# Linear attention and token/channel mixer on one core: two groups of input loads moved behind the transposing transfers of u in the SyncE queue

## The chip, the cores and the metric

One Trainium2 chip, one of its cores. The time is that of one execution on the device, in microseconds, and the kernel's time is the median of several executions. A profile of one execution gives what each engine did and when.

## What is computed

Eight batches, each of eight heads, 576 rows and head width 64. Linear attention with the feature map elu+1, then a mixer over rows and one over channels. Cut to what matters:

```python
phi = lambda x: np.where(x > 0, x, np.exp(x) - 1.0) + 1.0
kv  = einsum('bhsd,bhse->bhde', phi(k), v);  z = phi(k).sum(axis=2)
x   = einsum('bhsd,bhde->bhse', phi(q), kv) / (einsum('bhsd,bhd->bhs', phi(q), z) + 1e-6)
x   = x.transpose(0, 2, 1, 3).reshape(8, 576, 512)
h   = maximum(x.transpose(0, 2, 1) @ w_tok1, 0) @ w_tok2     # 576 -> 256 -> 576
u   = x + h.transpose(0, 2, 1)
out = u + maximum(u @ w_ch1, 0) @ w_ch2                      # 512 -> 1536 -> 512
```

## The kernel before, in words

A batch n passes through these steps, named as in the code. `load` (line 132) brings q, k and v of one batch from memory, each in two transfers of 576 KB, all issued by SyncE (SP). There are two sets of buffers for raw inputs, but the second is given over to sums of weights early on, so that from batch 2 on every batch uses the same three buffers (`rb`). `phi_exp` (L151, ScalarE), `phi_add` (L157, VectorE) and `phi_end` (L165, VectorE) make phi(q) and phi(k). `vcast` (L176) makes v bf16. `qtr_dma` (L221) is a transfer that transposes phi(q) into `qT`, in two halves. `kv` (L191 on TensorE) makes the small matrices. `nd_all` (L261 on TensorE, L270 to L290 on VectorE) makes x. `mm1` (L312) and `mm2` (L325) are the row mixer, and L337 on VectorE adds x to give u, two row groups at a time. `utr_dma` (L521) transposes u into `uT` by transfer, in two halves: `uta` after the first L337 of a batch, `utb` after the second. The 64 rows of each batch that fill no tile are kept for a pair of batches: `mm2_tails` (L346, with L350 on VectorE) makes `ut`, and `utr_tail_dma` (L526, step `utt`) transposes it into `uTt`.

The channel mixer of batch n is the large work of TensorE: `mm3` (L543), parts of it as `mix_one` (L723), the tail's part as `mm3_tail` (L557), then `pair_product` (L823) for the second matrix, by a scheme with seven block products instead of eight, whose sums are made on VectorE (`row_sums`, L666; `u_sums`, L700). `mm4` of the tail is L583. ACT takes the relu out of the accumulators (L550), and `pair_end` and `pair_put` add u and store.

The order of the work is written by hand. The outer loop goes over n, the batch whose channel mixer runs. `big` lists the pieces of that mixer, and `put(s, fn, ...)` hangs a step of another batch behind piece s: the row mixer of batch n+1, the feature maps of batch n+2, the loads of batch n+3. The list of steps is sorted by s and is stable, so steps of one s keep the order in which they were put. Every engine, and SP too, carries out its own instructions in this written order; an instruction that waits holds everything behind it on its queue. SP issues nearly all loads and all transposing transfers, on one DMA queue (q1 in the profile); POOL issues the stores of results (q0) in the middle of the run.

Two places matter here. The block for n=1 is written out before the loop; the one for n=2 is the first pass of the loop, with `b0 = 12`:

```python
put(16, load_all, 4, "q")          # n=1: ahead of todo["uta"], put at 19, and todo["utb"], at 24
put(25, load_all, 4, "kv")
...
put(b0 + 7, load_all, n + 3, "qv") # n=2: slot 19
at(b0 + 9, "mm2t")                 # slot 21: ut is made
at(b0 + 9, "utt")                  # slot 21: uTt is transposed
```

Of the kernel before, what the change touches and what calls it, by code (L numbers as in the profile page):

```python
# [19 lines left out]
def kernel(  # L20
# [844 lines left out]
    def m4s(n):  # L865
        return [lambda i=i, j=j: pair_product(n, i, j) for i in ORDER for j in range(2)]
# [133 lines left out]
    def steps(n):  # L1000

        out_ = [("kv", lambda: kv(n, range(2)))] if n < 2 else []
        if n == 1:
            puts = [nc.scalar.copy, nc.vector.tensor_copy if n == 1 else nc.scalar.copy]
            out_ += [(f"qt{c}", lambda c=c: qtr(n, c, puts[c])) for c in range(2)]
        for i, rs in enumerate(([0, 1], [2, 3], [4])) if n < 2 else ():
            for g in range(2):
                out_.append((f"nd{i}{g}", lambda g=g, rs=rs: nd(n, g, rs)))
        if n > 1:
            out_.append(("nd", lambda: nd_all(n)))  # L1010
        out_.append(("mm1", lambda: mm1(n)))
        if n > 1:
            out_ += [("mm2a", lambda: mm2(n, [0, 1])), ("mm2b", lambda: mm2(n, [2, 3]))]
            if n % 2:
                out_.append(("mm2t", lambda: mm2_tails(n // 2)))
            out_ += [("uta", lambda: utr_dma(n, [0, 1])), ("utb", lambda: utr_dma(n, [2, 3]))]
            if n % 2:
                out_.append(("utt", lambda: utr_tail_dma(n // 2)))
        return out_

    def run(bigs, fill):
        for i, big in enumerate(bigs):
            big()
            for s, fn in fill:
                if s == i:
                    fn()
        for s, fn in fill:
            assert s < len(bigs)
# [57 lines left out]
    put = lambda s, fn, *a: fill.append((s, lambda: fn(*a)))  # L1086
# [42 lines left out]
    put(24, todo["mm2b"])  # L1129
    put(24, todo["utb"])  # L1130
    put(24, pair_end, 1, "Z", 0, 0, 0)
    put(16, load_all, 4, "q")
    put(25, load_all, 4, "kv")
    put(26, pair_end, 1, "Y", 0, 1, 1)
    put(28, pair_end, 1, "X", 1, 0)
    put(28, pair_put, 1)
# [5 lines left out]
    for n in range(2, B - 1):  # L1142
        p, b = divmod(n, 2)
        tail = int(n == 3)
        mix = n in MIXED
        big = (m3x if mix else m3)(n) + m3t * tail + m4s(n) + m4(p, [8]) * tail
        b0 = 12 + 3 * tail
        todo = dict(steps(n + 1))
        fill = []
        put = lambda s, fn, *a: fill.append((s, lambda: fn(*a)))  # L1150
        at = lambda s, *nms: [put(s, todo.pop(nm)) for nm in nms if nm in todo]

        def phi_at(nm, ex, ad, en):
            for g in range(2):
                if ex is not None:
                    put(ex[g], phi_exp, nm, n + 2, 2 * g, 2)
            for g in range(2):
                put(ad[g], phi_add, nm, n + 2, 2 * g, 2)
                put(en[g], phi_end, nm, n + 2, 2 * g, 2)

        at(1, "nd")
        if n + 2 < B:
            if n > 3:
                phi_at("k", None, (2, 2), (3, 4))
                put(5, load_all, n + 3, "k")
            nm = "k" if n == 3 else "q"
            if mix:
                for which in (3, 4):
                    put(3, u_sums, which, tuc, b)
            if not mix:  # L1170
                phi_at(nm, (7, 7), (8, 9), (9, 10))
            else:
                for g in range(2):
                    put(3, phi_add, nm, n + 2, 2 * g, 2)
                    put(7, phi_exp, nm, n + 2, 2 * g, 2)
            put(10, *((qtr_dma, n + 2) if n != 3 else (load_all, n + 3, "k")))
            if n == 2:
                for g in range(2):
                    put(13, phi_add, "k", n + 2, 2 * g, 2)
        at(7, "mm1")  # L1180
        for s, k0 in ((7 if mix else 11, 0), (11 if mix else 12, 3)):
            for w in (1, 2):
                put(s, row_sums, n, w, k0, 3)
        if mix and n + 2 < B:
            for g in range(2):
                put(7 + 2 * g, phi_end, nm, n + 2, 2 * g, 2)
        if mix:
            for which in (1, 2):
                put(0, u_sums, which, tuc, b)
        if n == 3:  # L1190
            phi_at("q", (12, 13), (13, 13), (14, 14))
            put(15, qtr_dma, n + 2)
        at(13, "mm2a", "uta")
        put(14, row_sums, n, 3, 0, KH)
        put(b0 + 1, pair_copy, 0)
        if n == 2:
            for g in range(2):
                put(b0 + 1, phi_exp, "k", n + 2, 2 * g, 2)
                put(b0 + 2, phi_end, "k", n + 2, 2 * g, 2)
            put(b0 + 4, load_all, n + 3, "k")  # L1200
        at(b0 + 3 - tail, "mm2b", "utb")
        put(b0 + 4 - tail, row_sums, n, 4, 0, KH)
        put(b0 + 4 - tail, pair_end, n, "Z", 0, 0, 0)
        put(b0 + 5, pair_copy, 1)
        if n + 2 < B:
            for g in range(2):
                put(b0 + (5 if n == 2 else 2) + g, vcast, n + 2, g)
        put(b0 + 7, load_all, n + 3, "qv")
        put(b0 + 7, pair_copy, 2)
        if n > 2 and n + 3 < B:  # L1210
            put(b0 + 8, k_exp, n + 3)
        put(b0 + 9, pair_end, n, "X", 1, 1, 2)
        if n == B - 2:
            at(b0 + 6, "mm2t", "utt")
        at(b0 + 9, "mm2t")
        if n + 2 < B:
            put(b0 + 9, kv, n + 2, range(2))
        at(b0 + 9, "utt")
        put(b0 + 11, pair_end, n, "Y", 0, 1, 1)
        if n == B - 2:  # L1220
            for which in (3, 4):
                put(3, u_sums, which, tuc, b)
            put(1, first_sum)
            for which in range(1, 5):
                if which > 1:
                    put((3, 3, b0 + 2)[which - 2], first_sums, which)
                put(b0 + 10, u_sums, which)
        else:
            put(b0 + 13, pair_end, n, "X", 1, 0)
            put(b0 + 13, pair_put, n)  # L1230
        assert not todo, todo
        run(big, sorted(fill, key=lambda e: e[0]))
# [31 lines left out]
```

## Time and profile before

| What | Value |
|---|---|
| median of 8 executions | 250.29 us (249.14 to 251.64) |
| the profiled execution's own time | 250.17 us |
| its span in the profile | 248.4 us |
| TensorE (PE) busy | 237.1 us, 95% |
| VectorE (DVE) busy | 190.8 us, 77% |
| ScalarE (ACT) busy | 139.3 us, 56% |
| GpSimd (POOL) busy | 70.1 us, 28% |
| moved by DMA | 48.39 MB, mean 195 GB/s |
| mean granted TensorE clock | 0.996 |

The span is what the profile covers; 1.8 us of the execution's time lie outside it. A line of the timeline gives start, duration, engine, source line, operation and tiles, and in brackets how long the engine had been idle before it and what ended that. A line of waits gives the sum, the number and the longest. SPq is the issuing of a transfer by SyncE: its duration is not that of the transfer, and a merged line of two issues holds the pause between them. "Landing" is the time from the start of the issue to the last byte's report.

### The profile page before, as it was taken

The page shows a single profiled execution, that of the slowest core. Times are in us where ns is not written, and L with a number is a line of the kernel's source. Part 1 is how long each engine was busy: PE and PEld are TensorE (multiplying, and loading weights), DVE is VectorE, ACT ScalarE, POOL GpSimd, SP SyncE. Part 2 cuts the span into 40 slices and gives each one's busy share as a digit, 9 for nine tenths or more (in the row PEclk, how much of TensorE's full clock was granted, in tenths as well). Part 3 has the DMA queues.
Part 4 walks back from the last instruction along what each step waited for, and adds up shares of the span by engine and source line. Part 5 has one row for each costly group of instructions (what it writes and reads, how often), then busy time and mean ns, then how long its engine had stood idle before and what let it go on. Part 6 is the DMA issues. An engine that isn't in the chain of part 4 may idle for free.

```text
span 248.4 us, 5964 instructions
## 1 busy us (share of the span) xinstructions
PE 237.1 (95%) x2432; PEld 158.1 (64%) x2454; DVE 190.8 (77%) x330; ACT 139.3 (56%) x224; POOL 70.1 (28%) x84
## 2 busy tenths in 40 slices
PE   7699999999999799999899999999999999999993
PEld 3484455554877356875588545765577566888672
DVE  5954778897899698989894398858894879956853
ACT  4764791579765277736797168655952651275100
POOL 9770030496503600070004500051006800430000
PEclk9999999999999999999999999999999999999998
DMA  6999999999528992589949966699052702352036
GB/s 249 261 203 257 352 266 334 330 287 299 232 49 220 246 401 72 120 257 346 311 137 157 404 171 219 121 319 273 22 123 45 164 8 42 63 121 51 4 84 169
DMA packets 49771, 48.39 MB, mean 195 GB/s; under 512 B 30032, under 2 KB 35536, under 8 KB 49744
## 3 DMA queue, kind: packets, MB, share of 16 engines
q1 hardware_dynamic: 41648, 35.00, 48.1%
q0 software_dynamic: 7472, 12.22, 22.4%
q10 hardware_dynamic: 624, 0.79, 1.1%
q8 instruction: 19, 0.31, 0.5%
q14 instruction: 8, 0.07, 0.1%
HBM read 35.85 MB, written 9.44 MB: 182 GB/s over the span
## 4 chain that ended last, share of the span: by engine, by line
PE 59%; DMA 7%; DVE 3%; issue 1%; DVEq 0%
PE ps L823 19%; PE ps L543 15%; DMA uTt<-ut 5%; PE ps L751 4%; PE ps L777 4%; PE ps L312 3%; PE ps L325 3%; PE ps L723 3%; PE ps L570 2%; DMA uT<-u 2%; PE ps L592 2%; PE ps L261 1%; PE ps L191 1%; PE ps L557 1%; PE ps L583 1%
## 5 line engine op out<-in xcount | busy, mean ns | idle before, releaser
L543 PE MATMUL ps<-uT,wc 128*128 128x512 bf16 x284 | 66.5, 379 | 1.6 <-DMA uT<-u 1.3
L550 ACT ACTIVATE cr<-ps 128x512 bf16<-128x512 f32 x67 | 39.1, 600 | 35.6 <-PE ps L543 35.3
L543 PEld LDWEIGHTS <-wc 128*128 128x128 bf16 x288 | 27.3, 98 | 31.2 <-DMA uT<-u 1.8
L834 POOL TENSOR_TENSOR obuf<-obuf,q_raw 128x512 f32<-128x512 f32 x6 | 7.6, 1268 | 93.4 <-DVE obuf L832 60.8
L823 PE MATMUL ps<-k_raw,v_raw 128*128 128x256 bf16 x216 | 24.9, 273 | 0.0
L832 DVE TENSOR_TENSOR obuf<-ps,u 128x512 f32<-128x512 f32 x24 | 16.2, 687 | 10.4 <-PE ps L823 8.9
L823 PEld LDWEIGHTS <-cr 128*128 128x128 bf16 x216 | 21.0, 98 | 4.1
L823 PEld LDWEIGHTS <-v_raw 128*128 128x128 bf16 x216 | 21.0, 98 | 3.9 <-issue 0.4
L151 ACT ACTIVATE e<-q_raw 128x1152 bf16<-128x1152 f32 x16 | 18.3, 1161 | 7.2 <-DMA q_raw<-in_q_dram 7.2
L151 ACT ACTIVATE e<-k_raw 128x1152 bf16<-128x1152 f32 x16 | 18.2, 1165 | 3.5 <-DMA k_raw<-in_k_dram 3.5
L823 PE MATMUL ps<-wc,cr 128*128 128x256 bf16 x144 | 17.7, 273 | 0.0
L666 DVE TENSOR_TENSOR v_raw<-cr 128x768 bf16<-128x768 bf16 (+2 forms) x24 | 14.8, 619 | 3.6 <-ACT cr L729 2.1
L276 DVE TENSOR_TENSOR x<-ps,dens 128x768 bf16<-128x768 f32 x18 | 17.2, 954 | 0.4
L337 DVE TENSOR_TENSOR u<-ps,x 128x1024 bf16<-128x1024 f32 x12 | 14.7, 1222 | 1.9 <-PE ps L325 1.7
L312 PE MATMUL ps<-x,w 128*128 128x512 bf16 x49 | 13.4, 379 | 0.3
L176 ACT CAST vs<-v_raw 128x1152 bf16<-128x1152 f32 x12 | 13.5, 1163 | 0.0
L157 DVE TENSOR_SCALAR y<-k_raw 128x1152 bf16<-128x1152 f32 x16 | 11.7, 762 | 2.1 <-DMA k_raw<-in_k_dram 2.1
L165 DVE TENSOR_TENSOR qp<-e,y 128x1152 bf16<-128x1152 bf16 x16 | 11.9, 755 | 1.0 <-ACT e L151 0.3
L157 DVE TENSOR_SCALAR y<-q_raw 128x1152 bf16<-128x1152 f32 x16 | 12.3, 784 | 0.0
L834 POOL TENSOR_TENSOR obuf<-obuf,part 128x512 f32<-128x512 f32 x6 | 7.6, 1274 | 15.8 <-DVE obuf L832 15.8
L325 PE MATMUL ps<-ar,w2p 128*128 128x512 bf16 x44 | 11.8, 379 | 0.3
L165 DVE TENSOR_TENSOR kp<-e,y 128x1152 bf16<-128x1152 bf16 x16 | 11.7, 751 | 0.5 <-ACT e L151 0.4
(178 smaller groups left out, 428.6 us busy)
## 6 DMA issues: line engine op xcount, KB each, us to landing
k_raw<-in_k_dram SPq DMA_DIRECT2D x16, 576.0 KB, 6.1
q_raw<-in_q_dram SPq DMA_DIRECT2D x16, 576.0 KB, 6.3
v_raw<-in_v_dram SPq DMA_DIRECT2D x14, 576.0 KB, 10.0
out_dram<-obuf POOLq DMA_DIRECT2D x12, 512.0 KB, 6.6
wc<-in_moe_w_ch_dram POOLq DMA_DIRECT2D x8, 384.0 KB, 10.0
out_dram<-obuf POOLq DMA_DIRECT2D x4, 256.0 KB, 5.2
cr<-in_v_dram POOLq DMA_DIRECT2D x2, 288.0 KB, 7.5
out_dram<-obuf POOLq DMA_DIRECT2D x4, 128.0 KB, 7.5
```

Source lines behind the costliest of these rows:

```text
L151: nc.scalar.activation(out=e, in_=f, func=AF.Exp)
L157: nc.vector.tensor_scalar(out=y, in0=f, scalar1=1.0, scalar2=1.0, op0=ALU.add, op1=ALU.max)
L165: live["phi"] = nc.vector.tensor_tensor(out=dst.transpose([0, 2, 1, 3]), in0=e.rearrange("p (i t d) -> p i t d", i=nj, t=T), in1=y.rearran ...
L276: nc.vector.tensor_tensor(out=xv[:, :, rc0:rc0 + 3], in0=v_[m][:, :, k0:k0 + 6, 0:D].rearrange("p i (q a) d -> p i q a d", a=2), in1=den.r ...
L312: nc.tensor.matmul(out=ps[:, mt], lhsT=w1t[:, b, ms] if r == R else w1[:, r, ms], rhs=x[b][:, r, :], start=(r == 0), stop=(r == R))
L325: nc.tensor.matmul(out=ps[:, i], lhsT=w2v(kt, r, b), rhs=ar[b][:, kt, :], start=(kt == 0), stop=(kt == NT - 1 and not add))
L543: nc.tensor.matmul(out=ps, lhsT=wc1[:, kj, 128 * mc:128 * mc + 128], rhs=uTj[b][:, kj] if n < 2 else uT[b][:, :, kj], start=(kj == 0), sto ...
L550: nc.scalar.activation(out=cr[b][:, mc, :], in_=ps, func=AF.Relu)
L666: nc.vector.tensor_tensor(out=s_[which - 1][:, ks], in0=x_, in1=y_, op=op)
L823: nc.tensor.matmul(out=live[tile_][:, j], lhsT=lhs[:, k_], rhs=rhs[:, k_], start=(first and j == 0 and k_ == 0), stop=(k_ == KH - 1), skip ...
L832: nc.vector.tensor_tensor(out=o, in0=live[tile_], in1=u[n % 2][:, d::2, HC[c]], op=ALU.add)
L834: nc.gpsimd.tensor_tensor(out=o, in0=o, in1=part[i], op=ALU.add)
```

## The change

Two groups of loads go further back in SP's queue; no computation changes.

```diff
@@ block n=1
     put(24, todo["mm2b"])
     put(24, todo["utb"])
     put(24, pair_end, 1, "Z", 0, 0, 0)
-    put(16, load_all, 4, "q")
-    put(25, load_all, 4, "kv")
+    put(25, load_all, 4, "qkv")
     put(26, pair_end, 1, "Y", 0, 1, 1)
@@ loop, n from 2
-        put(b0 + 7, load_all, n + 3, "qv")
+        if n != 2:
+            put(b0 + 7, load_all, n + 3, "qv")
         put(b0 + 7, pair_copy, 2)
...
         at(b0 + 9, "utt")
+        if n == 2:
+            put(b0 + 9, load_all, n + 3, "qv")
         put(b0 + 11, pair_end, n, "Y", 0, 1, 1)
```

In the order of SP's instructions this is all that moves: in block n=1 the two loads of q of batch 4 go from ahead of the two transposes of u of batch 2 to behind both; in block n=2 the four loads of q and v of batch 5 go from ahead of the transpose of ut to behind it. PE, DVE, ACT and POOL keep their order.

## The prediction, made before the changed kernel was run

> **What bounds the kernel now.** I read the page first, then the waits of PE, then the timelines of PE and of SP's queue around each wait. PE is busy for 95% of the span at full clock, so only PE's idle time can be won. The waits of PE between 60 and 140 us are:
>
> ```profile
> PE ps L543 <- DMA uT<-u: 1.3, 1, 1.3
> PE ps L557 <- DMA uTt<-ut: 0.6, 1, 0.6
> PE ps L543 <- issue: 0.2, 1, 0.2
> ```
>
> So two transposing transfers hold PE up, once each. The chain of waits names the same two, with larger numbers:
>
> ```profile
> 78.88 5.21 DMA uT<-u
> 111.07 12.16 DMA uTt<-ut
> ```
>
> Those are whole transfers, from issue to landing. The second is almost wholly hidden: PE has other work until the last 0.6 us. What can be won is the idle time in brackets on PE's own timeline:
>
> ```profile
> 80.08 2.76 PE L583 MATMUL ps<-wc,crt 128*128 128x512 bf16 x11
> 84.14 1.90 PE L543 MATMUL ps<-uT,wc 128*128 128x512 bf16 x8 [1.30 <-DMA uT<-u]
> ...
> 122.05 0.60 PE L723 MATMUL ps<-q_raw,wc 128*128 128x256 bf16 x4
> 123.27 1.95 PE L557 MATMUL ps<-uTt,wc 128*128 128x128 bf16 x32 [0.62 <-DMA uTt<-ut]
> ```
>
> SP's timeline shows what stood in front of them:
>
> ```profile
> 75.13 1.13 SPq L132 DMA_DIRECT2D q_raw<-in_q_dram  x2
> 76.35 5.70 SPq L521 DMA_TRANSPOSE uT<-u  x2
> 82.15 1.04 SPq L132 DMA_DIRECT2D k_raw<-in_k_dram  x2
> ...
> 106.35 1.06 SPq L132 DMA_DIRECT2D k_raw<-in_k_dram  x2
> 107.46 2.48 SPq L132 DMA_DIRECT2D q_raw<-in_q_dram  x2
> 110.03 0.93 SPq L132 DMA_DIRECT2D v_raw<-in_v_dram  x2
> 111.07 1.26 SPq L526 DMA_TRANSPOSE uTt<-ut  x1
> ```
>
> By the tile views the two q loads (issued 75.13 and 75.8) took 5.4 and 6.4 us, so they landed at 80.5 and 82.2; the first half of uT, issued 76.35, took 6.9 and landed at 83.25; the second took 5.2 and landed at 84.10. Landings follow the order of issue, and the transposes came in 1 to 2 us after the last q. The DMA view of 76.6 to 80.6 us supports it: 431 of its 512 packets are of load size, though half a transpose had been asked for since 76.35.
>
> ```profile
> DMA packets 512, 1.01 MB, mean 251 GB/s; under 512 B 81, under 2 KB 81, under 8 KB 512
> ```
>
> (the counts by size are sums from below: 81 of the 512 are under 512 B, as a transpose's are). One merged SP line hides more: the second half's issue alone lasted 3.17 us (78.88 to 82.05), where the same issue takes 1.23 to 1.26 us behind an empty queue.
>
> **Part A, block n=1: q of batch 4 behind both halves of uT.** Nothing is added or removed. The two q issues (0.61 and 0.43 us) leave 75.13 and come after the second half.
> Step A1: the first half waits for u, whose first L337 ends at 74.57 + 1.22 = 75.79; it issues at about 75.85. The second waits for L337 ending at 77.64 + 1.22 = 78.86, as before.
> Step A2: with no load in front, its landing is read from the rows of other blocks: 3.1 and 3.1 us (101.69 and 105.0), 3.6 and 3.1 (157.26 and 159.66), 3.0 and 3.0 (182.9 and 185.1); the one at 131.79, close behind two transposes of q, took 5.1. The 159.66 row is nearest: a first half shortly before, q loads issued 1.35 us later. So 78.88 + 3.1 = 82.0, and 84.0 at worst. PE is free at 82.84. The stall of 1.30 us goes, with 0.8 us to spare; by the 5.1 us row only 0.1 of it goes.
> Step A3: what is late next? VectorE's L621 ends at 83.09 + 0.68 = 83.77 and frees a bank that L261 overwrites; L261 comes 1.83 us into PE's new run, at 84.67. The L700 sums (0.42 us each) then run from 83.77 to 84.65, and VectorE is free for L270 when L261 ends at about 85.4. From L270 on VectorE is nearly solid to 109 us, but that run is itself released by PE's L261, so it moves forward whole: PE gains nothing on it. The next half of uT lands at 105.02 + 3.1 = 108.1 against PE's need at 109.48; both move. A gives 1.30.
> Step A4, the price: q is issued at 78.88 + 1.25 = 80.1 and 80.8 instead of 75.13 and 75.8, about 5 us later; k and v behind it keep their place in the data, since all the bytes in front of v are the same. First reader of q:
>
> ```profile
> 91.41 1.42 DVE L157 TENSOR_SCALAR y<-q_raw 128x1152 bf16<-128x1152 f32 x2
> ```
>
> That will be 90.1 after the gain, the second half 90.8. Loads in this stretch took from 5.1 (k, 82.15) to 8.8 us (k's second, 82.75, beside POOL's stores issued from 82.51). So q's second half lands between 87.2 (6.4) and 89.6 us (8.8); I take 87.2, as its data goes ahead of most of the stores. Cost nil, covered by the VectorE work between landing and L157 (nd's L270 to L289 and two L700); if the cover went, each us of lateness first eats 0.88 us of VectorE's idle time (0.42 at 93.25, 0.46 at 98.03) and 1.4 us of uT's margin at 109.48, and then is PE's.
> k and v follow by about 1 us or less: v landed at 94.4 (83.8 + 10.6), read at 103.54; k at 91.5, read at 99.11. The next SP instruction, the transpose of q at 97.64, has an empty queue either way. POOL's queue has nothing moved past it; its stores only share the DMA engines.
>
> The Trainium skill, "DMA: Bandwidth & Descriptors", section "Rules for kernel authors", speaks against A: issue a DMA early and wait on its semaphore late. By that rule taken alone q's 5 us of lead are given away for nothing, and the sum would be 0 at best. The rows say that the lead is not used: q landed at 82.2 and is first read at 91.41, 9 us later, while uT landed 1.30 us too late. The rows decide: 1.30.
>
> **Part B, block n=2: q and v of batch 5 behind uTt.** Four issues of 0.4 to 2.0 us leave the place ahead of the transpose. They now queue behind its wait for ut, whose L350 ends at 106.98 + 1.38 = 108.36.
> Step B1: the transpose issues at 108.4 instead of 111.07, with only k in front, which landed at 107.0 + 5.8 = 112.8. Its own landing: 2.4 us with nothing near it (213.27), 6.7 behind q and v (164.21), so between 112.8 and 115.1. PE needs it at 122.65. The stall of 0.62 us goes with over 7 us to spare, if nothing else stands there: banks and relu of L557 are next. Its second group uses the bank that ACT's L729 empties at 122.74 + 0.59 = 123.33, and PE reaches it at about 123.5. So 0.62, with 0.2 us over.
> Step B2, the price: q issues at about 109.7 (or up to 111.6, if the transpose's issue takes the 3.17 us seen behind loads) instead of 107.46, and v some 2 to 4 us later than 110.03. q landed at 109.5 + 7.4 = 116.9 and would land at 119 to 121; its reader is L157 at 124.43, 122.5 after both gains. v landed at 122.8 and ends at about the same time, as the bytes are the same; its reader is at 128.84. Cost nil; with the cover gone, VectorE's idle times of 0.26 and 0.29 us after L157 are all there is to absorb it.
> k of batch 6 and later transfers keep their order, and wait for work of VectorE at 119.64, not for the queue.
>
> **Sum.** 1.30 + 0.62 = 1.92 us off the span, 248.4 to 246.5; the profiled execution goes from 250.17 to 248.25. The median of the eight was 0.12 above it: 250.29 becomes 248.4.
>
> **The rivals.**
> R1: only one part works. A fails if the transpose meets the 5.1 us row instead of the 3.1 us one: landing at 84.0, PE as late as before. Then only B is left: 250.29 - 0.62 = 249.7. For it: that row also had q loads behind it. Against it: two transposes of q were in front of it, where here the last one lands at 73.7 + 3.6 = 77.3, before the second half is asked for. If instead B's stall passes to the next wait (ACT's bank), A alone gives 249.0.
> R2: nothing. The transposes were slow for a reason other than the loads, or PE's gain is all taken back at the next dependence on VectorE, which is solidly busy from 98.5 to 109. Time 250.3. Against it: VectorE's run starts with PE's L261, and the landings follow the queue's order.
> R3, slower: q of batch 4 comes too late for L157 at 90.1, and VectorE, in order, holds back everything behind it: sums, relus and u. It breaks even where lateness exceeds 0.88 + 1.4 + 1.92 = 4.2 us, that is a landing at 94.3, 13.5 us after issue. The longest q load in the trace took 12.4 us, at the start beside the weights; v in this stretch took 11.5. A landing at 96.5 would give 252.5. It needs stores and loads to halve each other's rate for the whole stretch, and q stands ahead of k and v.
>
> **How the numbers follow.** The change as written, both stalls gone (247.9 to 248.9, with 248.4 likeliest): 0.64. Two small further gains or losses downstream are inside that. R1: A alone 0.07 (half of it over 0.5%), B alone 0.10. R2: 0.07. R3 or another late transfer: 0.12. About 0.5%, 1.25 us, is what a measurement of this kernel can tell from no change. So faster 0.64 + 0.035, about 0.68; same 0.035 + 0.10 + 0.07, about 0.20; slower 0.12. The range runs from 247.7 (below the main case's end, for the spread of 249.1 to 251.6 in single executions) to 250.0, which takes in both forms of R1; R3 and most of R2 lie outside.
>
> **What would show it.** Right: SP issues the second half of uT for about 1.25 us at 78.9; landings of 3.0 to 3.6 us; no DMA wait of PE at L543 or L557; L157's q line with no idle time before it. Wrong in A: a landing over 4 us. Wrong in R3's way: VectorE idle before L157 or ACT before L151 for a load of q. Gone elsewhere: new idle time of PE between 84 and 125 us, released by VectorE or ACT.

## The result, and the profile after

| | before | after |
|---|---|---|
| median | 250.78 us (33 runs, on the chips of this comparison) | 248.40 us (12 runs) |
| ratio of the comparison | | 0.9921, 95% interval 0.9900 to 0.9942 |
| span of the profiled execution | 248.4 us | 246.6 us |

The changed kernel is faster by 0.8%, 2.0 us of 250.78, clear of the 0.5% that can be told from no change. The medians lie 2.4 us apart; the 2.0 follow from the ratio, which leaves out slower executions of the kernel before, such as the four above 253 us.

The waits of PE between 55 and 140 us, where there were two for transfers, are down to one line, in the changed kernel's profile:

```profile
PE ps L543 <- issue: 0.2, 1, 0.2
```

PE's timeline at the two places. The brackets with the waits are gone, and L543 begins before the modelled end of L583 (80.50 + 2.76 = 83.26):

```profile
80.50 2.76 PE L583 MATMUL ps<-wc,crt 128*128 128x512 bf16 x11
83.10 1.89 PE L543 MATMUL ps<-uT,wc 128*128 128x512 bf16 x8
...
120.98 0.60 PE L723 MATMUL ps<-q_raw,wc 128*128 128x256 bf16 x4
121.42 1.95 PE L557 MATMUL ps<-uTt,wc 128*128 128x128 bf16 x32
```

SP's timeline shows the new order, and the loads right behind:

```profile
76.23 4.30 SPq L521 DMA_TRANSPOSE uT<-u  x2
80.62 1.06 SPq L132 DMA_DIRECT2D q_raw<-in_q_dram  x2
81.78 0.93 SPq L132 DMA_DIRECT2D k_raw<-in_k_dram  x2
...
105.29 1.06 SPq L132 DMA_DIRECT2D k_raw<-in_k_dram  x2
107.33 1.51 SPq L526 DMA_TRANSPOSE uTt<-ut  x1
108.89 1.08 SPq L132 DMA_DIRECT2D q_raw<-in_q_dram  x2
110.09 0.92 SPq L132 DMA_DIRECT2D v_raw<-in_v_dram  x2
```

The second half of uT was issued at 79.30 and landed after 3.1 us (5.2 before); uTt landed after 4.7 us (12.2 before). q of batch 4 landed at 84.9 and 86.8, and VectorE reaches it with no bracket, that is, without waiting:

```profile
90.36 1.42 DVE L157 TENSOR_SCALAR y<-q_raw 128x1152 bf16<-128x1152 f32 x2
```

Starts on PE give the account. From L583's start to L543's: 4.06 us before (84.14 - 80.08), 2.60 after (83.10 - 80.50), so 1.46 won. From the last L723 to L557: 1.22 before, 0.44 after, so 0.78 won. That is 2.24; PE reached L583 0.42 us later in this execution, which leaves 1.82 of span. From L557 to the end both profiles are the same to 0.01 us, since PE never waits there.

### The profile page after: what moved, and what is told of

Same layout as the page of the kernel before. It is cut to its first block, busy times and chain, and to the rows that moved or that the text cites. A ratio compares the mean times of both kernels' runs of the same rounds, so it can differ in the third digit from the quotient of the medians.

```text
span 246.6 us, 5963 instructions
## 1 busy us (share of the span) xinstructions
PE 237.7 (96%) x2432; PEld 158.6 (64%) x2454; DVE 190.6 (77%) x330; ACT 139.5 (57%) x224; POOL 70.4 (29%) x84
## 4 chain that ended last, share of the span: by engine, by line
PE 82%; DMA 11%; POOL 3%; issue 1%; DVE 1%; SPq 0%; POOLq 0%
PE ps L823 23%; PE ps L543 21%; DMA wc<-in_moe_w_ch_dram 7%; PE ps L312 6%; PE ps L583 5%; DMA q_raw<-in_q_dram 5%; PE ps L325 4%; PE ps L723 4%; PE ps L751 4%; PE ps L777 4%; PE ps L557 2%; PE ps L570 2%; PE ps L592 2%; PE ps L261 2%; PE ps L191 2%
## 5 line engine op out<-in xcount | busy, mean ns | idle before, releaser
L543 PE MATMUL ps<-uT,wc 128*128 128x512 bf16 x284 | 66.5, 379 | 0.3 <-issue 0.2
L543 PEld LDWEIGHTS <-wc 128*128 128x128 bf16 x288 | 27.4, 98 | 29.7 <-issue 0.9
L823 PE MATMUL ps<-k_raw,v_raw 128*128 128x256 bf16 x216 | 24.9, 273 | 0.0
L823 PEld LDWEIGHTS <-cr 128*128 128x128 bf16 x216 | 21.0, 98 | 4.1
L823 PEld LDWEIGHTS <-v_raw 128*128 128x128 bf16 x216 | 21.1, 98 | 3.9 <-issue 0.4
L823 PE MATMUL ps<-wc,cr 128*128 128x256 bf16 x144 | 17.7, 273 | 0.0
L157 DVE TENSOR_SCALAR y<-k_raw 128x1152 bf16<-128x1152 f32 x16 | 11.7, 763 | 2.3 <-DMA k_raw<-in_k_dram 2.3
L157 DVE TENSOR_SCALAR y<-q_raw 128x1152 bf16<-128x1152 f32 x16 | 12.3, 784 | 0.0
L583 PE MATMUL ps<-wc,cr 128*128 128x512 bf16 x47 | 11.8, 379 | 0.3 <-DMA wc<-in_moe_w_ch_dram 0.3
```

What stands on the lines that cost most here:

```text
L157: nc.vector.tensor_scalar(out=y, in0=f, scalar1=1.0, scalar2=1.0, op0=ALU.add, op1=ALU.max)
L543: nc.tensor.matmul(out=ps, lhsT=wc1[:, kj, 128 * mc:128 * mc + 128], rhs=uTj[b][:, kj] if n < 2 else uT[b][:, :, kj], start=(kj == 0), sto ...
L583: nc.tensor.matmul(out=ps, lhsT=crt[:, kc, :] if t == 8 else cr[b][:, kc, 128 * r:128 * r + 128], rhs=wc2[:, kc, :], start=(kc == 0), stop ...
L823: nc.tensor.matmul(out=live[tile_][:, j], lhsT=lhs[:, k_], rhs=rhs[:, k_], start=(first and j == 0 and k_ == 0), stop=(k_ == KH - 1), skip ...
```

## The experiments

All edits are to the changed kernel unless said otherwise. Each is timed beside the kernel before on the same chip. Starts on PE (L583 to L543, "the gap at L543": 4.06 before, 2.60 without a wait) are compared rather than spans, since the time before 80 us varies by some tenths.

**Each part alone, and both again.** `a_alone` has only the first edit of the diff, `b_alone` only the second.

> Part A only: q of batch 4 behind both halves of uT; q and v of batch 5 stay ahead of uTt. Theory (order in SP's queue, two independent stalls): PE's wait of 1.3 us at L543 is gone, PE's wait of 0.6 us at L557 stays; 1.3 to 1.5 us faster than before, ratio about 0.9945. Rival (the stalls are one delay handed on, so that a start 1.4 us earlier meets uTt that comes no earlier): the wait at L557 grows by up to 1.4 us to about 2.0, and the ratio is about 1.000.

> Part B only: q and v of batch 5 behind uTt; q of batch 4 stays ahead of uT. Theory: PE's wait of 1.3 us at L543 stays, that at L557 goes; 0.6 to 0.8 us faster than before, ratio about 0.997. Rival (the wait at L557 is also one for ACT's bank, which comes no earlier): at most 0.2 us, ratio 0.999 to 1.000.

> Both parts, beside each part alone on the same chip. Theory (independent): the sum of the two, 1.9 to 2.3 us, ratio 0.991 to 0.9925. Rival (they overlap): no better than part A alone, about 0.9945.

Measured on one chip, before at 250.96: part A alone 250.17, ratio 0.9960 (0.9937 to 0.9984); part B alone 250.04, 0.9963 (0.9935 to 0.9991); both 249.06, 0.9940 (0.9918 to 0.9963). The medians give 0.79 + 0.92 = 1.71 us for the parts and 1.90 for both: the parts add up, within the intervals. These are wide: that of both holds the theory's 0.9925 and the rival's 0.9945 alike, and only the first measurement of the change (0.9921) and a third one further down (0.9899) decide for the theory. In the profile of part B alone the wait at L557 is gone and 0.98 us of wait at L543 stays. But two profiles hold something neither theory expected. In that of part A alone, which is that of the slowest of its 22 executions (251.24), PE waits for both:

```profile
83.79 1.90 PE L543 MATMUL ps<-uT,wc 128*128 128x512 bf16 x8 [0.79 <-DMA uT<-u]
124.36 1.95 PE L557 MATMUL ps<-uTt,wc 128*128 128x128 bf16 x32 [2.06 <-DMA uTt<-ut]
```

The wait at L557 grew by 1.44 us, as the rival had it, though uTt did not merely come no earlier: issued at 110.98 it took 13.3 us, and came 1.1 later than in the kernel before. The trace has a fetch of instructions in it (queue q8, one packet of 16 KB), which began at 120.31 and held one of the sixteen DMA engines for 2.66 us. The transpose's last two completions came at 123.38, all others by 122.34, so the fetch accounts for 1.0 of the 1.1. And in the second profile of the changed kernel itself the wait at L543 is back, with no load in front:

```profile
84.06 1.90 PE L543 MATMUL ps<-uT,wc 128*128 128x512 bf16 x8 [0.88 <-DMA uT<-u]
```

The half of uT issued at 79.22 took 4.8 us there. The DMA views from 79.5 to 84 us of the two profiles of this one kernel differ in their counts and in one line, which is in the second only:

```profile
q8 instruction: 1, 0.02, 1.3%
```

A fetch again; it began at 81.98 us and held one DMA engine for 0.94 us, to 82.92. That is where the transpose was being finished: all its other completions came by 81.82, the last two at 82.93, right behind the fetch. Of the sixteen reports that make up the landing fifteen were in by 82.44, the last at 84.01. In the first profile the fetch came at 88.5. The kernel before has no fetch between 73 and 88 us, so its own wait at L543 is not of this kind.

**More and less in front of uT.** `half` leaves one of q's two loads in front, `double` both and k between the halves:

```diff
-    put(25, load_all, 4, "qkv")
+    put(16, load, "q", 4, 0)            # half
+    put(25, load, "q", 4, 1); put(25, load_all, 4, "kv")
+    put(16, load_all, 4, "q")           # double
+    put(23, load_all, 4, "k"); put(25, load_all, 4, "v")
```

> Part B kept; of q of batch 4 one load (half the bytes) ahead of both halves of uT as before, the other behind them. Theory (order in the queue, with a fixed time when PE comes): the one load is done by about 79.5 to 80.5 us, the halves of uT land by 80.5 to 81.5 and 82.0 to 82.6, PE waits 0 to 0.2 us: as fast as both parts within 0.3 us. Rival (delay in proportion to the bytes): half the wait, 0.6 us, stays.

> Part B kept; q of batch 4 ahead of both halves of uT as before, and k of batch 4 between the halves. Theory (order in the queue): the second half lands behind 1.18 MB more, at about 330 GB/s 3.6 us later, at 87 to 88 us; PE waits 4.5 to 5.5 us at L543; 2.5 to 3.5 us slower than before. Rival (sharing of the DMA engines, order without effect): the second half lands less than 2 us later than before, PE waits under 3.3 us, and the time is at most 1.3 us above before.

`half`: ratio 0.9919 (0.9889 to 0.9948), what the changed kernel has. One load in front delays the first half of uT (4.9 us instead of 3.1) and costs nothing that the time shows, because PE comes late enough; but the interval is too wide to exclude the rival's 0.6 us. Its profile has 0.99 us of wait at L543, and a fetch at 82.44. Fifteen of the sixteen reports of the second half were in by 82.94, the last, behind the fetch, at 84.50. PE would have gone on at 80.80 + 2.60 = 83.40: without the fetch there would have been no wait, as the theory has it. `double`: the second half landed 8.6 us after its issue at 79.70, at 88.3, and PE waited as the order of the queue has it:

```profile
88.32 3.59 PE L543 MATMUL ps<-uT,wc 128*128 128x512 bf16 x8 [4.66 <-DMA uT<-u]
```

The time, 255.36 against 251.13 (ratio 1.0169, 1.0108 to 1.0229), is 4.2 us worse, more than the 2.5 to 3.5 expected. The eight matmuls took 3.59 us instead of 1.89. The windows (PEclk is the third number from the end) show why:

```profile
82.00:87.00 5.00, 1.66 (x8) 0.57 (x6) 2.59 (x4) 0.00 (x0) 3.38 (x5) 0.93 1.19 283
87.00:92.00 5.00, 3.68 (x14) 1.19 (x16) 0.85 (x2) 0.65 (x2) 0.00 (x0) 0.50 1.03 384
92.00:94.00 2.00, 2.00 (x45) 1.43 (x42) 1.02 (x3) 0.55 (x1) 0.00 (x0) 0.73 0.89 353
```

After the long idle time PE was granted half its clock, from 86.3 to 93.1 us, which cost another 2.15 us between L543 and the last L723. The Trainium skill, "TensorE: Matmul & The Clock Gate", section "Part 1: The HAM clock gate", has the clock halved after an idle window of about 3.4 us; the rows agree in kind but not in size, as the clock fell 2.6 us after PE's last matmul (83.66). Stalls of up to 2.06 us in the other profiles (`a_alone`, `act_q`) kept the full clock.

**The same bytes on another queue.** `pool_q` has POOL issue q of batch 4, `act_q` ACT; k and v stay behind uT.

```diff
-    put(25, load_all, 4, "qkv")
+    for c in range(2):
+        put(16, load_pool, 4, "q", c)   # nc.gpsimd.dma_start; act_q: slot 24, nc.scalar
+    put(25, load_all, 4, "kv")
```

> Part B kept; the two loads of q of batch 4 issued in their old place (slot 16) but by POOL, so on another DMA queue than the transposes. Theory (the transposes wait for the bytes ahead of them in their own queue): the two queues take turns, the halves of uT land at about 80.5 and 82 to 82.9 us, PE waits 0 to 0.4 us, time within 0.4 us of both parts. Rival (any load in flight takes the DMA engines from the transposes): they land at 83.3 and 84.1 as before, PE waits 1.3 us, time that of part B alone (ratio 0.997).

> Part B; the two loads of q of batch 4 issued by ACT at about 77.4 us, so on another queue than the transposes and in flight beside both halves of uT. Theory (what delays a transpose is mainly the bytes ahead in its own queue): the second half lands 3.1 to 4.2 us after its issue (82 to 83.1), PE waits 0 to 0.3 us without a fetch. Rival (any load in flight delays it, by about its own bytes): it lands at 84 or later, PE waits 1.2 us or more as in the kernel before.

`pool_q`: no wait at L543, gap 2.60, ratio 0.9937 (0.9910 to 0.9965). But it does not tell what it was made for: POOL had nothing else to do and issued at 70.2, so q had landed by 76.6, before the halves of uT were in flight (both took 3.1 to 3.2 us). What those loads did hold up is the transpose of q in front: its issue at 73.80 lasted 2.90 us, until q was in, against 1.31 in the kernel before. `act_q` does tell: q was issued at 76.48 and 77.02, the halves of uT at 77.55 and 80.6.

```profile
86.64 1.90 PE L543 MATMUL ps<-uT,wc 128*128 128x512 bf16 x8 [2.06 <-DMA uT<-u]
```

The first half took 6.7 us, as behind q on SP's own queue (6.9), and landed 1.1 us after q's last byte. The second took 6.0, with a fetch at 84.5 in it; fifteen of its sixteen reports were in after 4.5 us, at 85.09, and PE could have gone on at 84.42, so 0.7 us of the wait is left without the fetch. This execution, 251.91, is the slowest of the run. Time 250.04, ratio 0.9973 (0.9950 to 0.9995), that of part B alone. The rival is right here, if smaller than it said: what delays a transpose is load data in flight, on whichever queue. The change works because q is asked for late enough, not because SP's queue is special.

**How late may q be?** `kqv` and `kvq` only change the order of the loads behind uT.

```diff
-    put(25, load_all, 4, "qkv")
+    put(25, load_all, 4, "kqv")         # or "kvq"
```

> Both parts, but batch 4 is loaded in the order k, q, v. Theory: q lands at 89 to 91 us, L157 at about 90.4 waits 0 to 0.7 us for it, absorbed by VectorE's idle time: the time is that of both parts within 0.3 us. Rival (VectorE has no slack there): what L157 waits shows in the time one for one.

> Both parts, but batch 4 is loaded in the order k, v, q, so that q comes last. Theory (the price of a late q as reckoned before the run: 0.88 us of VectorE's idle time and 1.4 us of uT's margin absorb the first 2.3 us): q lands at about 94.5, L157 waits about 4 us, PE loses about 1.8 us, so the time is about that of before. Rival (no slack): PE loses all 4 us and the time is about 2 us above before. Other rival (more slack than reckoned): PE loses under 0.8 us.

`kqv`: q landed at 90.7 and 93.3, later than expected, and L157 waited 1.34 us for its second load. PE from L543 to the last L723 took 37.83 us (37.88 after): absorbed. The median, 249.95, ratio 0.998 (0.9956 to 1.0004), is nevertheless 1.0 us above that of `half` on the same chip, where the theory allowed 0.3. The profiled execution, at 249.06 one of the fastest, does not show why. It had a fetch and lost 1.1 us at L543 (a gap of 3.71 instead of 2.60), which brought VectorE to L157 that much later; without a fetch the same landing would mean about 2.4 us of wait, more than there is room for (see the margin of 1.7 us below). That is an estimate from this profile, and no run shows it. `kvq`: q landed after 11.6 to 12.5 us and VectorE waited.

```profile
95.23 0.76 DVE L157 TENSOR_SCALAR y<-q_raw 128x1152 bf16<-128x1152 f32 x1 [4.96 <-DMA q_raw<-in_q_dram]
96.62 0.76 DVE L157 TENSOR_SCALAR y<-q_raw 128x1152 bf16<-128x1152 f32 x1 [0.63 <-DMA q_raw<-in_q_dram]
97.30 0.68 DVE L531 CUSTOM_DVE_ANT_0 cr<-ps,part 128x512 bf16<-128x512 f32 x1
```

PE then waited for the relus that stand behind L157 in VectorE's order:

```profile
98.04 0.60 PE L723 MATMUL ps<-q_raw,wc 128*128 128x256 bf16 x4 [2.38 <-DVE cr L531]
98.47 0.60 PE L823 MATMUL ps<-wc,cr 128*128 128x256 bf16 x4
100.37 1.89 PE L823 MATMUL ps<-wc,cr 128*128 128x256 bf16 x8 [1.30 <-DVE cr L531]
```

From L543 to the last L723 PE took 43.26 us instead of 37.88, a loss of 5.4 for a wait of 5.6. By PE's starts the two waits cost 4.0 us, so 1.6 of the 5.6 were absorbed, and a spell of half clock from 99.9 to 103.3 us, after idle times of 2.38 and 1.30, cost the other 1.4. Time 253.70, ratio 1.0107 (1.0032 to 1.0183), four executions: worse than the theory's "about that of before", and closest to the rival of no slack, though by way of the clock.

**The fetch, and whether its delay can be had out.** `both_third` is the changed kernel a third time. `gated` lets the first load of q wait until the second half of uT has landed; `pool_gate` loads q as `pool_q` does and lets k and v wait.

```diff
-        nc.sync.dma_start_transpose(                     # in utr_dma
+        live["uT_in"] = nc.sync.dma_start_transpose(
...
-    put(25, load_all, 4, "qkv")
+    put(25, load_behind, 4, "qkv")      # load(..., gate=live["uT_in"]) for the first
```

> The changed kernel a third time, beside the next three. Its first profile had no wait at L543, its second 0.88 us, with an instruction fetch of 16 KB (queue q8) in the DMA engines at 81.98 us, just where the second half of uT was being finished. Theory (the fetch holds up one of the sixteen shares of the transpose): where a q8 packet falls between 81 and 82.5 us, the half lands after 4.6 to 5.0 us and PE waits 0.8 to 1.0 us; where none does, 3.1 us and no wait; single times fall into two groups about 1 us apart. Rival (chance in the transposes themselves): landing and q8 packet have nothing to do with each other.

> Both parts, and the first load of q of batch 4 also waits until the second half of uT has landed, so that no load stands behind the transpose in the DMA engines. Theory (a fetch costs its own 0.94 us, and the loads queued behind the transpose make 1.7 of it): with a fetch the half lands after 3.9 to 4.3 us, PE waits 0 to 0.4 us; q lands by 87 to 89.5 us, before L157 at 90.2; as fast as the changed kernel's better group, 0.3 to 0.6 us better on the median. Rival (q comes too late): L157 waits for q and the kernel is slower than the changed one by what exceeds 1.3 us.

> Part B; q of batch 4 loaded by POOL's queue from about 70 us, as in the run pool_q, and k and v of batch 4 wait until the second half of uT has landed. Theory: no wait at L543, or at most 0.4 us with a fetch, and no late q: 0.3 to 0.6 us better than the changed kernel on the median. Rival (the fetch alone makes the whole delay): a wait of 0.8 to 1.0 us stays in about half of the runs and nothing is won.

`both_third`: 248.32, ratio 0.9899 (0.9864 to 0.9934); its profile has no fetch between 71.6 and 88.7, a landing of 3.1 us and no wait. With `after` and `both_again` that is three profiles of one kernel: fetch at 88.5 and 88.7, no wait; fetch at 81.98, 0.88 us. The profiles of `a_alone` (81.75) and `kqv` (81.89) have it as well, 4.7 and 4.9 us, and in both one report of the sixteen is late and the last completions come 0.01 us behind the fetch. But a fetch in a transpose is not always a delay. In `kvq` it began at 81.62 and the half landed in 3.1 all the same; and in eleven of the fourteen profiles a fetch begins 2.5 to 2.9 us after the issue of the half of uT at about 105 us, where ten landed in 3.1 and one in 4.7. What decides is open. The single times of `both_again` fall into six from 247.88 to 248.61 and eleven from 249.02 to 249.62, as expected, and those of `pool_q` into seven up to 248.36 and nine from 249.06. The first measurement of the change has no clear gap, and only one execution of each run is profiled: that the groups are those with and without a fetch is likely, and not shown.

`gated`: its single times fall into two groups, 247.74 to 248.57 and 251.19 to 251.79, and the profiled execution is of the slower one, so it shows the bad case. It had a fetch at 82.6, and with no load behind it the half of uT still took 4.7 us. So in this profile the fetch makes the whole delay, the loads behind it nothing, and the theory falls. q came late (1.68 and 0.71 us of wait at L157), which cost 0.80 at L823, and the next half of uT to be waited for also had a fetch in it and cost 1.03. Median 248.57, ratio 0.9931 (0.9887 to 0.9975), no better than the changed kernel. `pool_gate`: 249.68, ratio 0.9950 (0.9923 to 0.9977), a fetch at 81.3 and 1.10 us of wait at L543. Nothing was won, as the rival had it, but its reason is not shown, because the halves were late from the start:

```profile
71.95 6.68 SPq L221 DMA_TRANSPOSE qT<-qp  x2
```

The second of these two issues began at 73.88 and ended at 78.64, when POOL's q had landed (78.57). The halves of uT followed at 78.73 and 80.08 instead of 76.2 and 79.3; the fetch fell into the first (4.8 us), and the second took 4.3. No version was clearly faster than the changed kernel.

## Why the prediction was right

- The time: 248.4 was forecast, 248.40 measured; span 246.5 forecast, 246.6 measured. The gain of 1.9 us is what was reasoned, 2.0 measured. That the median agrees to a tenth is luck: the same kernel gave 249.06 and 248.32 in the two later measurements, and two terms below (0.32 and 0.42 us) nearly cancel in the span.
- Step A1 and A2: the second half of uT landed 3.1 us after its issue in two of three profiles. The row that the prediction put aside, 5.1 us for the half issued at 131.79, was read wrongly. It was laid to two transposes of q in front, but these had landed by 134.2. The DMA view of the kernel before from 133.5 to 137 us shows the fetch in it, with nothing moved from 134.7 to 135.2 and 6 to 12 GB/s from there to 136:

```profile
q8 instruction: 1, 0.02, 1.7%
```

  All fourteen profiles have a fetch in this half, and 5.0 to 5.7 us. So the worst case of R1 is no rare one: at L543 it is the 4.8 us of `both_again`, and costs the changed kernel 1.05 of A's 1.46 us when it comes (a gap of 3.65 instead of 2.60).
- Step A3: PE's run after L543 moved forward whole, 37.91 us before and 37.88 after from L543 to the last L723. No new wait.
- Step A, size: the stall was worth 1.46, not 1.30, and in B 0.78, not 0.62. The bracket counts from the modelled end of the last matmul, and without a stall the next one starts 0.16 us before that end. This 0.32 us was missed; the prologue of the profiled execution (0.42 later) hid it.
- Step A4: q landed at 86.8, where 87.2 was taken, and cost nothing. The cushion behind it was mis-sized: 2.3 us were reckoned from VectorE's idle time and uT's margin at 109.48. The nearest dependents are L531's relus. In the changed profile:

```profile
92.20 0.69 DVE L531 CUSTOM_DVE_ANT_0 cr<-ps,part 128x512 bf16<-128x512 f32 x1 [0.42 <-ACT part L731]
94.56 0.69 DVE L531 CUSTOM_DVE_ANT_0 cr<-ps,q_raw 128x512 bf16<-128x512 f32 x1
96.09 1.47 PE L823 MATMUL ps<-wc,cr 128*128 128x256 bf16 x12
```

  The second relu ends at 95.25, and PE's fifth matmul of L823, the first to use its rows, starts about 96.5 (it is where PE waits the second time in `kvq`): 1.3 us, and 0.42 of VectorE's idle time ahead of the first, 1.7 in all. `kqv` used 1.34 of it, and `gated` and `kvq` absorbed 1.6 each of the 2.4 and 5.6 us that they waited. The idle time of 0.46 at 98.03 and uT's margin come too late to help. R3's break-even would then be near 1.7 + 1.92 = 3.6 us of lateness, and the half clock makes it dearer beyond.
- Also in A4, v of batch 4 landed at 95.3 in the kernel before, not at 94.4 (its two loads took 10.6 and 11.5 us). k and v came 2.0 and 1.7 us later in the changed profile, not "about 1 us or less". Neither was waited for.
- The rule "issue early" lost against the rows as weighed: 5 us of q's lead were given up at no cost.
- Step B1: issued at 107.33, landed 4.7 us later at 112.0, against PE's need at 121.4. ACT's bank did not stand in the way.
- Step B2: q of batch 5 landed at 116.2, where 119 to 121 was taken, and v at 121.2; no reader waited for them.
- "Landings follow the order of issue" was right as a reading and too narrow as a reason: `act_q` shows the same delay by loads of another queue.

## What to carry to other kernels

Ahead of a transfer that an engine is about to wait for, look at which loads are in flight with it, and compare each load's landing with its first reader: here 9 us of slack stood in front of a transfer that came 1.3 us late. Moving the slack load behind costs nothing while its reader's margin holds; find that margin from the next instructions behind the reader on its own in-order engine that another engine waits for (1.7 us here), not from the engine's total idle time. A margin of 0.8 us on a transfer is not safe where a fetch can add 1.7, so profile such a kernel more than once.

## What was not expected of the hardware

A single instruction fetch of 16 KB, 0.94 us on one of sixteen DMA engines, delayed the landing of a transposing transfer from 3.1 to 4.7 to 4.9 us in five profiles; in others a fetch within a transpose delayed nothing. Why it comes near 82 us in one execution of a program and near 88 in another, and when it delays, was not found. A stall of 4.66 us took PE's clock to 0.50 for 6.8 us, so it cost nearly half as much again.
